# Token places written by indirect transfers into a DRAM table, a bias added by VectorE, and down products split for paired tiles only, in a Fourier-layer and mixture-of-experts kernel

## The chip, the cores and the metric

The kernel runs on one core of a Trainium2 chip. The metric is the time of one execution on the device in microseconds (us). The engines are named as in the profile: PE is TensorE with its matmuls, PEld its weight loads, DVE is VectorE, ACT is ScalarE, POOL is GpSimd, SP is SyncE, which here only issues transfers.

## The reference, cut to what matters

Eight sequences of 2496 rows and 256 columns go through a spectral layer: a real Fourier transform along the rows, a complex linear map with a bias, a soft threshold, and the transform back. The 19968 rows that come out then go, each for itself, through one of eight experts, chosen by the largest of eight logits.

```python
X = np.fft.rfft(x, axis=1)
Yr = Xr @ w_r - Xi @ w_i + b_r
Yi = Xr @ w_i + Xi @ w_r + b_i
Yr = np.sign(Yr) * np.maximum(np.abs(Yr) - lam, 0.0)   # Yi likewise, lam = 0.01
y = np.fft.irfft(Y, n=x.shape[1], axis=1)

logits = x @ w_gate                                    # x is y as (19968, 256)
e_idx = np.argmax(logits, axis=1)
gate_w = probs[np.arange(N), e_idx]                    # softmax of the logits
eom = 1.0 / (1.0 + np.exp(-(x @ w_output_gate)))
for e in range(E):
    mask = e_idx == e
    h = np.maximum(x[mask] @ w1[e], 0.0)               # 256 to 1024
    out[mask] = gate_w[mask, None] * eom[mask, e, None] * (h @ w2[e])
```

## The kernel before, in words

**Numbers.** Values are kept in float32 and split before a product into two float16 parts, high and low. A product of two such values is three float16 products (high-high, high-low, low-high), which is why so many steps come as a copy on ACT (the high part) and a subtraction on DVE or POOL (the low part).

**The Fourier part, batch by batch.** 2496 = 39 x 64. For each of 8 batches: `stage1` (L618) multiplies by the 39-point transform and L627/L628 split the result into `at`; `load_a` turns it round, by DMA transposes or by PE (`turn_a`, L661); `stage2` (L696) is the 64-point transform, split by L707/L708 into `xt` with a negated copy (L710 or L711). `mix` is the complex linear map: 24 matmuls (L726) into one bank of 512 columns, preceded by one matmul that puts the bias into that bank (L720: constant selector times the bias in two float16 parts, `b16`, made on POOL by L564 to L567, with the threshold already added). Two instructions make the soft threshold: ACT takes relu(y - 2 lam) from the bank (L741), DVE takes min(y, that) (L742), in the shifted form that the added threshold allows. The result `z` is split (copy L744 on ACT or L745 on POOL, subtraction L746 on POOL or DVE) and goes through the first step back (L756). There are 10 such `mix` blocks a batch, 80 in all. `inverse` transposes by DMA, `stage4` (L822) does the last step, and the rows go to a DRAM table `yd` together with a factor for each row (L834). `logits`, `gate` and `rank` (L867 to L960) pick each row's expert and its rank among that expert's rows.

**Expert weights.** While the batches run, `weights` reads the experts' matrices, splits them (L1017 to L1022) and stores them as float16 pairs in DRAM (`wd`).

**Routing, in two phases.** The tokens are laid out in tiles of 128 rows of one expert. Phase 0 makes the first 64 tiles out of the first four batches, as 32 pairs; phase 1 makes the other 99 single tiles once all batches are ranked. Each batch has 22 columns of 117 tokens. For a column, DVE writes two one-hot tables, `ol` (L1217: place within the tile, 117 x 128) and `ob` (L1221: which tile, times the token's number, 117 x 64 or 117 x 99), and one matmul (L1248) adds their product to a map of 128 places by 64 or 99 tiles in PSUM. `indices` (L1152 to L1180, DVE) turns the maps into `gidx`, the rows to fetch, and `sidx`, the rows to write. Phase 0 has 88 columns, phase 1 has 176.

**The experts.** For each tile POOL gathers 128 rows of `yd` by `gidx` (L1321, an indirect transfer), the rows are scaled and split (L382 to L393, L1335, L1340, L1341), turned by a DMA transpose, multiplied by the first matrix ("up", L1448: 48 matmuls a block, in four steps for a pair and two for a single tile), relu and split (L1458 on ACT, L1459 on DVE), multiplied by the second ("down", L1413: 24 matmuls a tile, in two halves, each as soon as its half of `hh` is there), scaled (L1430) and scattered to the output by `sidx` (L1433). `fetch` loads a block's 2 MB of weights into one of three buffers (L1307), in two parts, up and down, and each part only when the expert changes; a part is issued when the block three places earlier has done with it.

**What sets the order.** The kernel is recorded by a planner (`Issue`): each step is a generator that yields an engine, a rank, a duration and the instructions; whenever an engine is free in the plan, the waiting step of lowest rank is taken. Ranks and durations are written-out constants (`P`, `Z1`, `QV` and so on). The chip then executes each engine's instructions in just that order, each waiting by semaphores for what it needs. A list in a `yield` offers a step to two engines, and the first that is free in the plan takes it.

## Time and profile before

| | |
|---|---|
| three timed runs | median 1487.54 us (1483.97 to 1492.78) |
| the profiled execution | 1490.97 us, with a span of 1489.1 us from its first to its last instruction and a mean granted PE clock of 0.986 |
| PE busy | 1425.2 us, 96% of the span |
| DVE, ACT, POOL busy | 1023.4, 738.7 and 582.0 us |
| first expert product (L1448) | starts at 571.61 us |
| first single tile | up starts at 925.5 us |

A row of the profile's page names line, engine, operation, what is written and read, and a count; after the bar stand the busy time of the group, the mean duration of one in ns, and the time that the engine sat idle just before them, with what ended it. In a timeline a row is a start in us, a length, the instruction and how many follow each other; in brackets is the idle time before it. Matmuls overlap: one lasts about 0.27 us from its start to its end, but the next starts after about 0.11 us, so the pitch from one row's start to the next row's is what PE pays.

### The profile page before, as it was taken

What the parts mean: (1) busy time and instruction counts of PE and PEld (TensorE: products, weight loads), DVE (VectorE), ACT (ScalarE), POOL (GpSimd) and SP (SyncE); (2) the same over time, 40 slices, a digit from 0 to 9 for tenths busy, and PEclk for the clock granted to TensorE, in tenths of its full rate; (3) what the DMA queues carried; (4) which work ended last, traced back from release to release, by engine and by line L of the source; (5) the groups of instructions that cost most, each with busy time, mean ns of one, the idle gap of its engine ahead of it and who ended that gap; (6) DMA issues with size and microseconds to landing.
All of it is one profiled execution on the core that took longest, in us unless ns stands there. A gap on an engine that the chain in (4) does not pass through costs nothing. (4 is left out here: it accounts for less than half of the span.)

```text
span 1489.1 us, 42875 instructions
## 1 busy us (share of the span) xinstructions
PE 1425.2 (96%) x16464; PEld 1288.6 (87%) x16464; DVE 1023.4 (69%) x3167; ACT 738.7 (50%) x1415; POOL 582.0 (39%) x659
## 2 busy tenths in 40 slices
PE   5999999999989999999999999999999999999998
PEld 5998888898878777789998889889898988989898
DVE  4888778789999988789888865445454544545432
ACT  4777777777666655343333343333343333333332
POOL 2264645536354445333333343334333333333311
PEclk8999999999999999999999999999999999999999
DMA  7778989898777678978775778583847568386420
GB/s 191 175 166 222 219 224 220 216 210 209 188 193 187 157 207 198 260 194 234 220 235 158 205 228 273 133 237 80 235 115 194 152 158 225 86 238 196 110 51 23
DMA packets 294136, 276.39 MB, mean 186 GB/s; under 512 B 241859, under 2 KB 250426, under 8 KB 282155
## 3 DMA queue, kind: packets, MB, share of 16 engines
q1 hardware_dynamic: 277369, 229.59, 59.3%
q0 software_dynamic: 15872, 42.83, 10.2%
q8 instruction: 129, 2.11, 0.6%
q10 hardware_dynamic: 690, 1.24, 0.3%
q14 instruction: 76, 0.62, 0.1%
HBM read 337.35 MB, written 58.91 MB: 266 GB/s over the span
## 5 line engine op out<-in xcount | busy, mean ns | idle before, releaser
L1448 PE MATMUL ps<-eT,wbuf 128*128 128x128 f16 (+1 forms) x6288 | 485.0, 233 | 18.3 <-DMA wbuf<-wd 18.1
L1413 PE MATMUL ps<-wbuf,hh 128*128 128x256 f16 x3912 | 482.1, 275 | 1.9 <-issue 1.9
L1448 PEld LDWEIGHTS <-wbuf 128*128 128x128 f16 x6288 | 432.2, 98 | 44.3 <-DMA wbuf<-wd 20.9
L1413 PEld LDWEIGHTS <-hh 128*128 128x128 f16 x3912 | 376.1, 99 | 44.9 <-issue 2.2
L1459 DVE SCALAR_TENSOR_TENSOR hh<-ps,hh 128x512 f16<-128x512 f32 x326 | 224.8, 690 | 250.3 <-ACT hh L1458 201.8
L1458 ACT ACTIVATE hh<-ps 128x512 f16<-128x512 f32 x326 | 193.5, 594 | 296.3 <-PE ps L1448 277.2
L1433 POOL DMA_INDIRECT out<-o,sidx x163 | 164.2, 1007 | 304.8 <-ACT o L1430 111.4
L1321 POOL DMA_INDIRECT yg<-yd,gidx x163 | 160.4, 984 | 292.7 <-DVE yhl L1341 223.7
L726 PE MATMUL ps<-whl,xt 128*128 128x256 f16 x1920 | 227.2, 276 | 0.0
L726 PEld LDWEIGHTS <-xt 128*128 128x128 f16 x1920 | 190.1, 99 | 33.8 <-issue 1.3
L1340 ACT ACTIVATE yhl<-yg,ys 128x256 f16<-128x256 f32 x163 | 82.2, 505 | 183.2 <-DMA eT<-yhl 90.8
L1341 DVE SCALAR_TENSOR_TENSOR yhl<-yg,ys,yhl 128x256 f16<-128x256 f32 x163 | 78.5, 482 | 89.2 <-ACT yhl L1340 89.2
L1430 ACT ACTIVATE o<-ps,fac 128x256 f32<-128x256 f32 x163 | 77.0, 472 | 82.4 <-PE ps L1413 72.9
L746 POOL TENSOR_TENSOR zhl<-z,zhl 128x512 f16<-128x512 f32 x62 | 73.0, 1179 | 56.5 <-ACT zhl L744 52.4
L618 PE MATMUL ps<-f1t,x 117*128 117x120 f32 (+1 forms) x704 | 90.9, 287 | 0.0
L618 PEld LDWEIGHTS ps<-f1t,x 117*128 117x128 f32 (+1 forms) x704 | 87.8, 203 | 2.0 <-ACT at L627 0.6
L745 POOL CAST zhl<-z 128x512 f16<-128x512 f32 x47 | 29.7, 631 | 137.8 <-DVE z L742 83.5
L756 PE MATMUL ps<-gt,zhl 128*128 128x128 f16 x960 | 66.5, 219 | 10.2 <-POOL zhl L746 4.1
L756 PEld LDWEIGHTS <-zhl 128*128 128x128 f16 x960 | 58.5, 98 | 18.8 <-POOL zhl L746 4.9
L1221 DVE TENSOR_SCALAR ob<-t,blk,va 117x99 f16<-117x99 f16 (+1 forms) x264 | 71.7, 337 | 0.0
L741 ACT ACTIVATE zhl<-ps,sc 128x512 f32<-128x512 f32 x80 | 54.7, 684 | 30.3 <-PE ps L726 23.9
L822 PE MATMUL ps<-bdt,f4t 120*117 120x512 f16 x264 | 69.1, 379 | 0.4 <-ACT ste L773 0.3
(193 smaller groups left out, 1684.6 us busy)
## 6 DMA issues: line engine op xcount, KB each, us to landing
wbuf<-wd SPq DMA_DIRECT2D x262, 1024.0 KB
yd<-yt SPq DMA_DIRECT2D x120, 158.4 KB
x<-in_x SPq DMA_DIRECT2D x114, 156.0 KB
wr<-in_moe_w SPq DMA_DIRECT2D x32, 512.0 KB
wd<-wsp SPq DMA_DIRECT2D x64, 256.0 KB
yg<-yd,gidx POOLq DMA_INDIRECT x163
eT<-yhl SPq DMA_TRANSPOSE x163
out<-o,sidx POOLq DMA_INDIRECT x163
```

The lines of the kernel that those rows point to most:

```text
L618: T.matmul(pv[:, dh, :, m * j:m * j + m], xs[:k, j0 + j, 128 * dh:128 * dh + 128], fw, start=True, stop=True)
L726: T.matmul(yp[:, 256 * j:256 * j + 256], xt_[:, v, 2 * dh + j, 64 - 64 * u:192 - 64 * u], whl[:, dh, vw, 256 * u:256 * u + 256], start=Fal ...
L756: T.matmul(bv[:, j], zhl[:, vz, c:c + 128], gt[:, 2 * p + j, v], start=(n == 0), stop=(n == 2))
L1321: yield "G", r + 5.6 * t - 30, 1.0, lambda: G.indirect_dma_start(out=yg, out_offset=None, in_=src, in_offset=bass.IndirectOffsetOnAxis(ap= ...
L1340: yield "A", r - 10, 0.5, lambda: A.activation(yhl[:, 0], yg[:, :256], AF.Copy, scale=s)
L1341: yield "D", r - 10, 0.48, lambda: V.scalar_tensor_tensor(yhl[:, 1], yg[:, :256], s, yhl[:, 0], ALU.mult, ALU.subtract)
L1413: T.matmul(st["pt", t][1][:, :256], hh[:, v, fc, 128 * n:128 * n + 128], w[:, fc // 2, vw, fc % 2], start=(half == k == 0), stop=(half == ...
L1430: yield "A", r - DN, 0.47, lambda: A.activation(o, pt[:, :256], AF.Copy, scale=fac)
L1433: yield "G", r - DN, 1.0, lambda: G.indirect_dma_start(out=out, out_offset=bass.IndirectOffsetOnAxis(ap=sidx[:, t:t + 1], axis=0), in_=o, ...
L1448: T.matmul(pt[:, 128 * m * j:128 * m * (j + 1)], w[:, dh, g // 4, vw, 128 * (g % 4):128 * (g % 4) + 128], eT[:, :m, v, dh], start=(n == 0) ...
L1458: yield "A", r, 0.6, lambda: A.activation(hv[:, 0], pt, AF.Relu)
L1459: yield "D", r, 0.69, lambda: V.scalar_tensor_tensor(hv[:, 1], pt, 0.0, hv[:, 0], ALU.max, ALU.subtract)
```

## The change

1. **Bias.** The matmul L720 and its selector are gone, and so are POOL's two-part bias. DVE adds the bias, as float32, while it empties the bank (`z` = bank x 2^-7 + bias). As there is no shift any more, the soft threshold takes one more instruction: ACT makes relu(z - lam) into `c`, and then either DVE takes min(z + lam, `c`), or ACT makes relu(-z - lam) and POOL subtracts it from `c`.
2. **Phase 0 of the routing** (`SCAT`). DVE computes for each token the address of its place (`addr` = place x 64 + tile, or a number out of bounds for a token that phase 0 leaves out), and POOL issues 88 indirect transfers, one for each column, that write the tokens' numbers, 4 bytes each, into a table of 8192 numbers in DRAM, which was filled with "none" before. SP reads the table back into `sidx` when all have landed, and one DVE instruction makes `gidx`. For phase 0 there are no one-hot tables, no matmuls L1248 and no `indices`.
3. **Phase 1** still uses one-hot tables, but four columns are written by one DVE instruction each for `ol` and `ob`, and the token's number is multiplied in by a third, on DVE or POOL.
4. **Single tiles.** The halves of a tile's down product are issued as one step of 24 matmuls that waits for both halves of `hh`; a pair still has two halves. The ranks of single tiles' up and down steps move with that.
5. The tables of constants change (ranks and planned durations), the values table comes as float16 within another constant, and `z` and `zhl` are given out by free place rather than in turn.

```diff
-P = 68.49
+P = 68.76
-Z3 = 40.87
+Z3 = 32.19
...
+SCAT = (0,)
+SG = 1.0
...
-            G.tensor_scalar(bs, bias, sc[:, 0:1], sc[:, 1:2], ALU.mult, ALU.add)
-            G.tensor_copy(b16, bs)
-            for p in (32, 96):
-                G.tensor_tensor(b16[p:p + 32], bs[p:p + 32], b16[p:p + 32], ALU.subtract)
...
+        yield "G", r + 5, 0.5, lambda: G.tensor_scalar(bs, bias, sc[:, 0:1], 1.0, ALU.mult, ALU.mult)
...
-            T.matmul(yp.rearrange("p (a d) -> p a d", a=2), sel, st[b, "bs"].rearrange("p (o d) -> p o d", o=1).broadcast_to([128, 2, D]), start=True, stop=False)
...
-        i, yp = yield "P", r, 2.85, f, True
+        i, yp = yield "P", r, 2.64, f, True
...
-        yield "A", r - Z1, 0.69, lambda: A.activation(c, yp, AF.Relu, bias=sc[:, 2:3], scale=2.0 ** -7)
-        yield "D", r - Z1, 0.68, lambda: V.scalar_tensor_tensor(z, yp, 2.0 ** -7, c, ALU.mult, ALU.min)
+        yield "D", r - Z1, 0.68, lambda: V.scalar_tensor_tensor(two(z), two(yp), 2.0 ** -7, bs, ALU.mult, ALU.add)
         io.free(i)
+        yield "A", r - Z1, 0.68, lambda: A.activation(c, z, AF.Relu, bias=sc[:, 1:2])
...
+            A.activation(z, z, AF.Relu, bias=sc[:, 1:2], scale=-1.0)
+
+        yield [("D", r - Z1 + QD, 0.85, lambda: V.scalar_tensor_tensor(z, z, sc[:, 1:2], c, ALU.subtract, ALU.min)), ("A", r - Z1 + QA, 0.68, f)]
+        if way:
+            yield "G", r - Z1, 1.25, lambda: G.tensor_tensor(z, c, z, ALU.subtract)
...
+        V.tensor_scalar(t2[:, 1], t2[:, 1], -none, none - 1, ALU.mult, ALU.add)
+        yield
+        V.scalar_tensor_tensor(t2[:, 0], rlo[:, cs], float((T_A, T_B)[ph]), t2[:, 0], ALU.mult, ALU.add)
+        V.tensor_tensor(addr[:, cs], t2[:, 0], t2[:, 1], ALU.add)
...
+    def scatters(ph, r):
...
+        def f(c):
+            i = G.indirect_dma_start(out=tab[ph], out_offset=bass.IndirectOffsetOnAxis(ap=addr[:, c:c + 1], axis=0), in_=tok[:, c:c + 1], in_offset=None, bounds_check=128 * n - 1, oob_is_err=False).ins
+            tc.declare_no_dep(i, group=key, reason="places of different tokens differ")
...
+        for c in range((NA, B)[ph] * NQ):
+            yield "G", r, 1.0, lambda: f(c)
+            r += SG
+        yield 3.0
+
+        def g():
+            d = nc.sync.dma_start(sidx[:, t0:t0 + n], tab[ph].rearrange("(p t) o -> p (t o)", p=128)).ins
+            for i in all_:
+                tc.add_manual_dep(d, i.name, mybir.DependencyInfo(mybir.DependencyClass.Sync, mybir.DependencyReason.DATA), reason="the table is whole")
+
+        yield "S", r, 0.5, g
+        yield 2.0
+        yield "D", r, 0.4, lambda: V.scalar_tensor_tensor(gidx[:, t0:t0 + n], sidx[:, t0:t0 + n], none, sidx[:, t0:t0 + n], ALU.is_lt, ALU.mult)
...
-                    for j in range(m):
-                        V.tensor_scalar(ol[:, j], iota[:P3], rlo[:, c0 + j:c0 + j + 1], None, ALU.is_equal)
...
+                yield "D", r, 0.147 * m, lambda: V.tensor_tensor(ol[:, :, :m], iota[:P3, :, :m], bc(rlo, 128), ALU.is_equal)
+                yield "D", r, 0.115 * m, lambda: V.tensor_tensor(ob[:, :, :m], iota[:P3, :n, :m], bc(blk, n), ALU.is_equal)
...
+        yield either("D", r, 0.11 * m, "G", r + QO, 0.7, lambda e: e.tensor_tensor(ob[:, :, :m], ob[:, :, :m], vb, ALU.mult))
...
-            io.go(up(t, m, half, w, eT, ie, hh, r + UP * half))
+            io.go(up(t, m, half, w, eT, ie, hh, r + UP * half * (m - 1)))
...
-            io.go(down(t + i, m, i, w, hh, ih, r + (5.6 + UP * i) * m + DN))
+            io.go(down(t + i, m, i, w, hh, ih, r + (11.2 + 2 * UP * i + DN if m > 1 else 4)))
...
-        for half in range(2):
-            for i in range(m * half, m * half + m):
+        for half in range(m):
+            for i in range(2 * half, 2 * half + 2):
                 yield "hh", t0, i
```

The order of the built programs shows the two places that matter most. First, POOL's order around batch 6's bias, at the beginning of phase 0's tables; `zhl` and `z` belong to the mix, `wr` and `wsp` to the experts' weights, `yt` to the rows that go to `yd`. Before:

```order
L1020 TENSOR_SCALAR wr_5345<-wr_5345,swe_6362 128x512
L1021 TENSOR_TENSOR wsp_6372<-wr_5345,wsp_6372 128x512
L564 TENSOR_SCALAR bs_6293<-bias,sc_6292 128x256
L565 CAST b_6294<-bs_6293 128x256
L567 TENSOR_TENSOR b_6294<-bs_6293,b_6294 32x256 x2
L746 TENSOR_TENSOR zhl_6409<-z_6408,zhl_6409 128x512
L1020 TENSOR_SCALAR wr_5942<-wr_5942,swe_6362 128x512
L1021 TENSOR_TENSOR wsp_6472<-wr_5942,wsp_6472 128x512
L745 CAST zhl_6453<-z_6452 128x512
```

And of the changed program (L561 is the bias, L1181 a scatter into the table, L743 the new subtraction, L745 and L746 as before, L1022 and L1023 the weights, L834 as before):

```order
L1181 DMA tab_78<-tok,addr 8192x1
L561 TENSOR_SCALAR bs_6435<-bias,sc_6434 128x256
L1022 TENSOR_SCALAR wr_5515<-wr_5515,swe_6466 128x512
L1023 TENSOR_TENSOR wsp_6557<-wr_5515,wsp_6557 128x512
L1181 DMA tab_78<-tok,addr 8192x1 x2
L743 TENSOR_TENSOR z_6426<-zhl_6427,z_6426 128x512
L1181 DMA tab_78<-tok,addr 8192x1
L746 TENSOR_TENSOR zhl_6427<-z_6426,zhl_6427 128x512
L1181 DMA tab_78<-tok,addr 8192x1 x11
L743 TENSOR_TENSOR z_6824<-zhl_6825,z_6824 128x512
L834 COPY yt_135<-gf_6593 117x4
L745 CAST zhl_6825<-z_6824 128x512
```

The 88 scatters stand between POOL's other instructions, one to eleven at a time, in 44 runs, from here to the last batch's mix; behind the last of them SP's read of the table stands in SP's queue ahead of one store of weights, the first loads of expert weights and the last batch's rows. Second, ACT's order among the single tiles, which follows PE's (`hh` empties a bank of an up step, `o` one of a down product, `yhl` prepares a later tile). Before:

```order
L1458 ACTIVATE hh_9932<-ps_20505 128x512
L1340 ACTIVATE yhl_20571<-yg_19893,ys_20603 128x256
L1458 ACTIVATE hh_9932<-ps_20574 128x512
L1430 ACTIVATE o_20652<-ps_20555,fac_19228 128x256
L1458 ACTIVATE hh_9932<-ps_20627 128x512
L1340 ACTIVATE yhl_20693<-yg_20015,ys_20725 128x256
L1458 ACTIVATE hh_9932<-ps_20696 128x512
L1430 ACTIVATE o_20774<-ps_20677,fac_19350 128x256
```

And now:

```order
L1514 ACTIVATE hh_9860<-ps_20201 128x512
L1514 ACTIVATE hh_9860<-ps_20234 128x512
L1514 ACTIVATE hh_9914<-ps_20263 128x512
L1514 ACTIVATE hh_9914<-ps_20309 128x512
L1486 ACTIVATE o_20403<-ps_20337,fac_18963 128x256
L1398 ACTIVATE yhl_20367<-yg_19711,ys_20373 128x256
L1398 ACTIVATE yhl_20428<-yg_19771,ys_20438 128x256
L1486 ACTIVATE o_20471<-ps_20378,fac_19146 128x256
```

Before, the two up steps of a tile alternated with the two halves of the tile before it; now the four up steps of two tiles follow each other, and then the two tiles' down products.

More of the change, by code (lines that the diff above doesn't have):

```diff
@@ L294, in tile_fft_moe @@
     pools = {}
+    tab = [pd.tile([128 * n, 1], I32, name=f"tab{ph}") for ph, n in enumerate((T_A, T_B))]
     turn = {}
@@ L442, in tile_fft_moe @@
     G.memset(oh16, 0.0)
[L443 removed]
+    rlo = pc.tile([P3, NCOL], F16, name="rlo")
     rhi = pc.tile([P3, NCOL], F16, name="rhi")
     io = Issue(list(range(8)))
[L447 removed]
+    slots = {k: Slots(n) for k, n in dict(x=XR - 6, s1=S1, A=AN, xt=3, bt=1, bd=1, yt=YR, ol0=OL[0], wr=WR - 1, wsp=SR, ol1=OL[1], fac=12, dg=1, gL=1).items()}
     slots.update({k: Places(range(EARLY[k])) for k in EARLY})
[L449 removed]
+    slots.update(eT1=Places([]), hh1=Places([]), z=Places(range(2)), zhl=Places(range(ZR)))
     give = lambda k: io.give(slots[k])
@@ L1031, in tile_fft_moe @@
     eb = pc.tile([128, T_ALL], F32, name="eb")
-    blk = pc.tile([P3, NCOL], F32, name="blk")
+    blk = pc.tile([P3, NCOL], F16, name="blk")
     def prefix(src, name):
@@ L1205, in routing @@
         io.set("blocks", ph)
+        if ph in SCAT:
+            yield from scatters(ph, r)
         pool = (psm, pools.get("h"))[ph]
-        for b in range(nb):
+        for b in range(0 if ph in SCAT else nb):
             for q in range(0, NQ, CB):
@@ L1227, in routing @@
                 yield max(gap * m - 1.2, 0.0)
-        while st.get(("cols", ph), 0) < nb * NQ:
-            yield 1.0
-        yield from parts(indices(ph), "D", r, 0.6)
+        if ph not in SCAT:
+            while st.get(("cols", ph), 0) < nb * NQ:
+                yield 1.0
+            yield slots["gL"]
+            yield from parts(indices(ph), "D", r, 0.6)
+            give("gL")
+            for i in range(-(-nb // (512 // n))):
+                io.free(route["map", ph, i][0])
         io.set("ix", ph)
-        for i in range(-(-nb // (512 // n))):
-            io.free(route["map", ph, i][0])
         if ph == 0:
```

190 lines of the change are left out of this document (104 added, 86 removed).

## The prediction

> **What bounds the kernel now.** I read first the page's busy times, then the busy time of each engine in five stretches, then the waits of PE over the last stretch. The page:
>
> ```profile
> span 1489.1 us, 42875 instructions
> PE 1425.2 (96%) x16464; PEld 1288.6 (87%) x16464; DVE 1023.4 (69%) x3167; ACT 738.7 (50%) x1415; POOL 582.0 (39%) x659
> ```
>
> PE is busy 96% of the span, so the end moves only by PE work that goes and by PE's idle time, 63.9 us in all. The stretches show where that lies: batches before any routing table, batches with phase 0's tables, the last batch's end, pairs, single tiles. After the bounds and the length come busy times, the granted PE clock, the DMA share and GB/s.
>
> ```profile
> 40.00:383.40 343.40, 339.11 (x3929) 302.45 (x3928) 282.66 (x697) 256.50 (x485) 171.87 (x212) 1.00 0.86 206
> 383.40:541.30 157.90, 146.54 (x1613) 124.48 (x1611) 149.90 (x439) 100.24 (x191) 68.34 (x87) 0.97 0.74 184
> 541.30:571.40 30.10, 26.56 (x281) 21.78 (x279) 25.90 (x73) 20.87 (x45) 15.90 (x19) 1.00 0.70 217
> 571.40:917.00 345.60, 343.30 (x3268) 304.71 (x3267) 275.75 (x1072) 137.43 (x269) 129.18 (x135) 1.00 0.77 218
> 917.00:1489.10 572.10, 547.53 (x7244) 513.42 (x7241) 271.80 (x840) 205.70 (x397) 188.91 (x190) 0.98 0.56 152
> ```
>
> The first stretch loses 4.3 us, the pairs 2.3. Phase 0's tables lose 11.4 while DVE is busy 95% of the stretch; the single tiles lose 24.6 with every other engine under half busy. The waits of PE in the single tiles say for what:
>
> ```profile
> PE ps L1448 <- DMA wbuf<-wd: 18.1, 8, 3.2
> PE ps L1413 <- issue: 1.9, 2, 1.0
> ```
>
> So three quarters of that loss is eight waits for the next expert's weights.
>
> **The bias off PE.** PE's rows around one mix, each a start, a length and what follows:
>
> ```profile
> 41.73 0.38 PE L720 MATMUL ps<-b,t 128*128 128x512 f16 x1
> 41.95 2.78 PE L726 MATMUL ps<-whl,xt 128*128 128x256 f16 x24
> 44.57 0.61 PE L661 MATMUL ps<-t,at 128*128 128x128 f16 x8
> 45.01 0.83 PE L696 MATMUL ps<-ct,A 128*128 128x128 f16 x12
> 45.68 0.38 PE L720 MATMUL ps<-b,t 128*128 128x512 f16 x1
> ```
>
> Matmuls overlap, so the price is the step to the next start: 0.22 us for L720, not its 0.38. Eighty of them go: **-17.6**. The same rows give 2.62 us for a mix of 24 (0.109 each), 0.055 for a turning matmul and 0.056 for stage 2. The order has eight more turning matmuls, 280 for 272: **+0.4**.
>
> **Phase 0's tables off PE and DVE.** Groups of the second stretch; after the bar stand busy time, mean ns, and the idle time before them:
>
> ```profile
> L1248 PE MATMUL ps<-ob,ol 117*128 117x64 f16 x88 | 10.5, 191 | 7.5 <-DVE ob L1221 7.1
> L1221 DVE TENSOR_SCALAR ob<-t,blk,va 117x64 f16<-117x64 f16 x88 | 28.7, 388 | 0.0
> L1217 DVE TENSOR_SCALAR ol<-t,rlo 117x128 f16<-117x128 f16 x88 | 23.4, 326 | 0.0
> ```
>
> With the 88 matmuls go 7.5 us of waiting for DVE and whatever they occupied, at most their busy 10.5: between 7.5 and 18.0. By the step of 0.055 for 128 columns above, 88 of them occupied some 4.5 of the 10.5; **-12**. DVE gets back 52.1 us there.
>
> **A dearer threshold.** The nearest rows to the new instructions (counts, then ns min/median/max; L742 from 40 to 383 us, the others over the whole run):
>
> ```profile
> L742 DVE SCALAR_TENSOR_TENSOR z<-ps,zhl x53: 669/690/693, 45.6 to 378.2; 128x512 f32<-128x512 f32 x53
> L1022 DVE SCALAR_TENSOR_TENSOR wsp<-wr,swe,wsp x14: 736/904/1540, 106.7 to 523.9; 128x512 f16<-128x512 f32 x14
> L744 ACT ACTIVATE zhl<-z x33: 613/629/667, 46.9 to 563.7; 128x512 f16<-128x512 f32 x33
> L746 POOL TENSOR_TENSOR zhl<-z,zhl x62: 1148/1158/1522, 47.6 to 569.1; 128x512 f16<-128x512 f32 x62
> L746 DVE TENSOR_TENSOR zhl<-z,zhl x18: 678/693/1660, 80.8 to 564.9; 128x512 f16<-128x512 f32 x18
> ```
>
> The bias addition takes L742's place at its 0.68. The second half of the threshold is new: in the order 41 of the 80 go to DVE and 39 to ACT with a subtraction on POOL. DVE's min reads two SBUF operands as L1022 does; I take 0.95, a little over its median. Of the 80 mixes 53, two thirds, have L742 in the first stretch: 27 x 0.95 = 26 us more on DVE; and of the low-part subtractions 33 are DVE's in the new order, not 18, ten of the fifteen there, at 0.69 to 1.0: 9 more. DVE goes from 282.7 to 317 us of a stretch that shrinks by 53 x 0.22 = 11.7 to 332: 95%, as full as it was in the second stretch. There PE's idle time beside that before L1248 was 11.4 - 7.5 = 3.9 us. ACT's 39 further instructions (0.63 each, 24.5) lie in its idle 87 us there. A mix's chain also grows by one instruction, which the waiting banks must cover. The cost lies between 0, if PE always has another batch's work to take, and 16, if it waits 0.3 us, about half of an L742, at each of the 53; **+7**, from the 4 us in 158 that the second stretch shows at the same filling (8.5 in 343, 4 more than now) and 3 for the longer chain. In the second stretch DVE loses 52 and gains some 13: 111 of about 141, so it is no longer the one that is late. What is late next is POOL.
>
> **The scatters on POOL.** The nearest rows are the gathers, also 128 rows by index; the first four rows give start, length, and in brackets the idle time before them, the fifth all gathers from 650 to 850 us, and the sixth the busy times there.
>
> ```profile
> 558.26 1.17 POOL L746 TENSOR_TENSOR zhl<-z,zhl 128x512 f16<-128x512 f32 x1
> 559.58 0.97 POOL L1321 DMA_INDIRECT yg<-yd,gidx  x1 [0.16 <-DMA wbuf<-wd]
> 560.86 0.95 POOL L1321 DMA_INDIRECT yg<-yd,gidx  x1 [0.30 <-issue]
> 562.12 1.21 POOL L1321 DMA_INDIRECT yg<-yd,gidx  x1 [0.30 <-issue]
> L1321 POOL DMA_INDIRECT yg<-yd,gidx x36: 967/981/1034, 653.5 to 846.6; - x36
> 650.00:850.00 200.00, 199.71 (x1926) 179.15 (x1924) 176.83 (x710) 75.79 (x146) 72.45 (x73) 1.00 0.69 205
> ```
>
> One indirect transfer holds POOL for 0.98 us whatever is written, with 0.15 ahead of a first and 0.30 between two in a row. The order puts the 88 scatters in 44 runs: 88 x 0.98 + 44 x 0.15 + 44 x 0.30 = 106 us. Between the first and the last of them stand POOL's other instructions, priced by these groups of the second stretch:
>
> ```profile
> L1021 POOL TENSOR_TENSOR wsp<-wr,wsp 128x512 f16<-128x512 f32 x17 | 20.3, 1195 | 1.4
> L746 POOL TENSOR_TENSOR zhl<-z,zhl 128x512 f16<-128x512 f32 x15 | 17.4, 1157 | 8.1 <-ACT zhl L744 7.3
> L1020 POOL TENSOR_SCALAR wr<-wr,swe 128x512 f32<-128x512 f32 x17 | 12.7, 746 | 14.5 <-ACT wsp L1017 14.0
> L745 POOL CAST zhl<-z 128x512 f16<-128x512 f32 x11 | 6.9, 629 | 39.6 <-DVE z L742 32.7 <-PE ps L822 6.0 <-PE ps L756 0.7
> ```
>
> Fifteen subtractions of the mix (17.4), five casts (3.1), nine pairs for the weights (17.5), two more weight parts (2.4) and fifteen small ones (4.5): 45 us. With 5 for the last landing, the table's reading and `gidx`, the chain lasts 156. PE's work between the same places: 157.9 less 12 and less 20 biases (4.4) is 141.5, and by the order more matmuls stand between them now, 51 of the mix (5.6), 30 of stage 2 (1.7) and others (1.6): about 150. So POOL is 6 us late on this estimate: **+6**, between 0 and 20 (a pitch of 0.16 more, one launch's idle time, for each scatter). Who waits for a late POOL: each mix's step back L756, through the low part, and at the end the pairs' first gathers. Behind SP's read of the table wait a store of weights, the first expert weights and the last batch's rows; behind `gidx` on DVE, the last batch's emptying of banks. A scatter also waits, by the order's semaphores, for the eighth before it; at 1.2 us each that leaves it 9.6 us. The nearest transfers, the last two scatters of the output, land much sooner (start, length):
>
> ```profile
> 1477.46 2.60 DMA out<-o,sidx
> 1482.76 2.13 DMA out<-o,sidx
> ```
>
> The Trainium skill, page "SBUF — State Buffer", section "SBUF: two separate sides", has VectorE and GpSimd share a port that one holds for a whole instruction, and has transfers issued by GpSimd take some 3.1 us rather than 0.62 beside a VectorE copy. The trace disagrees: 967 to 1034 ns for 36 gathers with DVE busy 88% of the time. By the page's figure the scatters' chain would be an estimated 88 x 3.1 + 50 = 323 us, 173 late. As a mechanism priced from rows it stands in the third rival below.
>
> **Phase 1.** Its edits fall into 571 to 917, where PE is busy 343.3 of 345.6, and its maps are needed only when the singles begin. DVE has 70 us free there to cover them: nothing. If a table came late, the pitch of a single tile, some 5.8 us (572 / 99), would be the price.
>
> **Single tiles.** A change of expert, as SP, PE and the clock show it:
>
> ```profile
> 975.42 0.36 SPq L1307 DMA_DIRECT2D wbuf<-wd  x1
> 983.66 1.50 PE L1448 MATMUL ps<-eT,wbuf 128*128 128x128 f16 x24
> 997.14 1.07 PE L1448 MATMUL ps<-eT,wbuf 128*128 128x128 f16 x16 [2.71 <-DMA wbuf<-wd]
> 1064.00:1066.00 2.00, 2.00 (x21) 1.69 (x19) 1.16 (x3) 1.70 (x4) 1.01 (x1) 0.63 0.98 396
> 1066.00:1068.00 2.00, 2.00 (x15) 1.57 (x13) 1.59 (x8) 0.56 (x2) 0.98 (x1) 0.52 0.64 165
> ```
>
> The load issued at 975.42 serves the wait that ends at 997.14: 21.7 us for three blocks' parts. After a wait the clock falls to 0.52 to 0.63, which costs 4 x 0.425 = 1.7 us, seen after five of the eight: 18.1 + 8.5 = 26 in all. The buffers come free by PE's order. Before, up and down halves alternate, and the lead of the first load is 8.2 us. In the new order four ups and then two downs follow each other, so that the up part comes free two halves earlier: by 24 or 32 matmuls of 0.09 to 0.11, a lead of 10.4 to 11.3, against stalls of 2.3 in the mean (18.1 / 8). So they shrink to nothing or to 2 us each, as the down parts come later in turn. Between 0 and 26 off; **-8**, a third. The relu of two tiles in a row has ACT's free 64% to hide in. At the very end two tiles now finish 2.6 us apart (24 matmuls), and each one's scatter takes an issue of 1.0 and 2.1 to 2.6 to land: **+1**.
>
> **The sum.** -17.6 + 0.4 - 12 + 7 + 6 - 8 + 1 = -23.2. The profiled execution took 1490.97, 3.4 above the median of the runs: 1467.8, or **1464** against 1487.5.
>
> **Rivals.** *Nothing in the way*: POOL keeps pace, DVE's filling costs 2, and more than half of the weight waits goes (-15): -17.6 + 0.4 - 15 + 2 - 15 + 1 = -44, **1443**. For it: POOL's lateness is 4% of its chain, and the lead grows by more than the mean wait. Against: the down parts come later by what the up parts gain. *Handed back*: DVE at 95% and POOL in series hold each mix. With the scatters' pitch at 1.45, their chain is 22 us longer, which takes back nearly all: **1486**. For it: both engines stand in one chain with every mix, and L746 has maxima of 1.5 on POOL and 1.7 on DVE. *Slower, by the scatters*: POOL is held at each scatter by DVE, or by the eighth before it, whose 117 writes of 4 bytes are slow to land. The trace has no write of 4 bytes. It decides from a pitch of 1.56: 106 / 88 = 1.20, and 31 us more (the 23 gained and the 7.4 of the bound below) over 88. If each scatter waits out one DVE instruction of 0.68, the pitch is 1.88, 60 us more than at 1.20; PE has other batches' work for some 9 of it: 1464 + 51 = **1515**. For it: nothing in 650 to 850. Against: those gathers beside a DVE that is 88% busy. *No effect*: the order shows that L720 and phase 0's L1248 are gone, so hardly.
>
> **How the numbers follow.** What a measurement of this kernel can tell from no change is about 0.5%, 7.4 us: faster is under 1480, slower over 1495. Chances: the forecast (1452 to 1478) 0.47, nothing in the way 0.18, handed back 0.19, slower by the scatters 0.14, no effect 0.02. Faster is the first two and 0.01 of handed back, 0.66; the same is 0.16 of handed back and no effect, 0.18; slower is 0.14 and the last 0.02 of handed back, 0.16. The range goes from the first rival, 1443, to 1492, above handed back; the slower case is left out, and what lies below 1443.
>
> **What would show it.** Right: no idle time of PE over 8 us before 383; scatters at about 1.2 us pitch, with POOL some 90 to 95% busy between the first and the last; PE's idle time around the first gathers under 10; weight waits of 8 to 12 us in sum; the singles' stretch shorter by 5 to 10. Wrong: PE waiting for `zhl` low parts or for DVE's `z` by tens of us; scatters above 1.5 us; the first pair later than 560 us; weight waits as before.

## The result, and the profile after

| | before | after |
|---|---|---|
| four timed runs each, median | 1489.14 us | 1550.98 us (1546.42 to 1554.95) |
| ratio | | 1.0419, 95% interval 1.0389 to 1.0449 |
| span of the profiled execution | 1489.1 us | 1553.2 us |

The change made the kernel slower by 62 us. The page of the changed kernel, as of before:

```profile
span 1553.2 us, 42607 instructions
PE 1436.4 (92%) x16304; PEld 1294.5 (83%) x16304; DVE 1011.6 (65%) x2790; ACT 763.5 (49%) x1471; POOL 722.1 (46%) x774
```

PE has less to do, yet is busy 11 us longer, at a granted clock of 0.965 for 0.986, and its idle time went from 63.9 to 116.8 us. To see where, the span is cut at the first pair's first matmul and at the first single tile: batches from 350 us, pairs with what is left of the batches, single tiles. Busy times of PE, PEld, DVE, ACT and POOL follow the length; then come PE's clock, the DMA share and GB/s. Before:

```profile
350.00:571.60 221.60, 204.89 (x2288) 173.74 (x2286) 207.31 (x594) 144.21 (x279) 104.50 (x132) 0.98 0.76 190
571.60:925.50 353.90, 351.60 (x3345) 312.24 (x3344) 281.02 (x1088) 140.95 (x276) 132.28 (x139) 1.00 0.77 220
925.50:1489.10 563.60, 539.03 (x7166) 505.79 (x7163) 266.33 (x823) 201.99 (x389) 185.61 (x187) 0.98 0.55 150
```

After:

```profile
350.00:598.00 248.00, 204.31 (x2079) 170.50 (x2077) 191.24 (x442) 159.73 (x309) 184.00 (x193) 0.88 0.70 168
598.00:987.40 389.40, 371.04 (x3372) 326.15 (x3369) 261.24 (x849) 143.74 (x282) 168.70 (x177) 0.96 0.71 203
987.40:1553.20 565.80, 536.88 (x7166) 502.88 (x7163) 266.19 (x823) 199.58 (x389) 183.56 (x186) 0.99 0.55 149
```

The first pair comes 26 us later, the pairs take 36 us more, the single tiles 2. In the first stretch DVE is no longer full (77% for 94%), and POOL has taken its place. From the first scatter to the last it is busy 140.5 of 178.4 us, and another 21.6 are the 0.15 to 0.3 us ahead of each scatter, 91% in sum:

```profile
382.00:560.40 178.40, 151.15 (x1545) 127.69 (x1543) 130.08 (x279) 115.27 (x221) 140.45 (x143) 0.89 0.69 156
```

```profile
L1181 POOL DMA_INDIRECT tab<-tok,addr x88 | 93.6, 1063 | 21.6 <-issue 20.2
```

What PE waits for from 350 to 598 us, with the sum, the count and the longest in us:

```profile
PE ps L756 <- ACT z L739: 6.3, 1, 6.3
PE ps L756 <- issue: 6.1, 9, 1.5
PE ps L715 <- issue: 5.8, 8, 1.0
PE ps L822 <- issue: 4.6, 3, 2.8
```

"Issue" is idle time for which the trace shows no reason. In pieces of over 0.25 us it sums to 27 us over the span; before it was 3.

### The profile page after: what moved, and what is told of

It is laid out like the page before. It is cut to its first block, busy times and chain, and to the rows that moved or that the text cites. A ratio compares the mean times of both kernels' runs of the same rounds, so it can differ in the third digit from the quotient of the medians.

```text
span 1553.2 us, 42607 instructions
## 1 busy us (share of the span) xinstructions
PE 1436.4 (92%) x16304; PEld 1294.5 (83%) x16304; DVE 1011.6 (65%) x2790; ACT 763.5 (49%) x1471; POOL 722.1 (46%) x774
## 5 line engine op out<-in xcount | busy, mean ns | idle before, releaser
L1504 PE MATMUL ps<-eT,wbuf 128*128 128x128 f16 (+1 forms) x6288 | 469.1, 233 | 11.9 <-DMA wbuf<-wd 7.6
L1470 PE MATMUL ps<-wbuf,hh 128*128 128x256 f16 x3912 | 461.6, 274 | 12.0 <-issue 5.9
L1504 PEld LDWEIGHTS <-wbuf 128*128 128x128 f16 x6288 | 423.6, 98 | 37.8 <-DMA wbuf<-wd 8.9
L1470 PEld LDWEIGHTS <-hh 128*128 128x128 f16 x3912 | 381.7, 99 | 60.8 <-issue 10.3
L715 PE MATMUL ps<-whl,xt 128*128 128x256 f16 x1920 | 233.8, 280 | 8.3 <-issue 5.8
L1181 POOL DMA_INDIRECT tab<-tok,addr x88 | 93.6, 1063 | 21.6 <-issue 20.2
L756 PE MATMUL ps<-gt,zhl 128*128 128x128 f16 x960 | 71.6, 226 | 20.9 <-ACT z L739 6.3
L743 POOL TENSOR_TENSOR z<-zhl,z 128x512 f32<-128x512 f32 x39 | 50.6, 1299 | 80.4 <-ACT z L739 54.7
L822 PE MATMUL ps<-bdt,f4t 120*117 120x512 f16 x264 | 71.8, 396 | 5.1 <-issue 4.6
L687 PE MATMUL ps<-ct,A 128*128 128x128 f16 x960 | 69.9, 225 | 3.0 <-issue 2.0
L382 DVE TENSOR_REDUCE ym<-yg 128x1 f32<-128x256 f32 x163 | 66.5, 410 | 6.1 <-DMA yg<-yd,gidx 6.1
```

The source lines that it names most:

```text
L715: T.matmul(yp[:, 256 * j:256 * j + 256], xt_[:, v, 2 * dh + j, 64 - 64 * u:192 - 64 * u], whl[:, dh, vw, 256 * u:256 * u + 256], start=(n ...
L756: T.matmul(bv[:, j], zhl[:, vz, c:c + 128], gt[:, 2 * p + j, v], start=(n == 0), stop=(n == 2))
L1181: i = G.indirect_dma_start(out=tab[ph], out_offset=bass.IndirectOffsetOnAxis(ap=addr[:, c:c + 1], axis=0), in_=tok[:, c:c + 1], in_offset= ...
L1470: T.matmul(st["pt", t][1][:, :256], hh[:, v, fc, 128 * n:128 * n + 128], w[:, fc // 2, vw, fc % 2], start=(fc == k == 0), stop=(fc == 7 an ...
L1504: T.matmul(pt[:, 128 * m * j:128 * m * (j + 1)], w[:, dh, g // 4, vw, 128 * (g % 4):128 * (g % 4) + 128], eT[:, :m, v, dh], start=(n == 0) ...
```

## The experiments

The theories, as the expectations number them: **1**, the scatters are the loss, either (1a) because PE's instructions come late while POOL issues a long run of indirect transfers, or (1b) because POOL is late with its other work; **2**, the dearer threshold on ACT, DVE and POOL; **3**, the order that the new constants give.

Times are medians; the kernel before took 1486 to 1490 us beside every set. The sets ran on different chips, which turned out to matter: the first result and two sets (E1 to E4, E13 to E16) came from chips on which PE has such unexplained idle time, three sets (E5 to E8, E9 to E12, E17 and E18) from chips on which no run shows more than the 1.4 us of E8. The changed kernel itself ran on one of these three, in E12, and shows none. Below they are called chips with and without **slow stretches**.

**E1, E14, E18: phase 0's tables by one-hot products again.** The scatters are gone, all else is as changed.

```
-SCAT = (0,)
+SCAT = ()
```

> The changed kernel with phase 0's tables made by one-hot products again; everything else as changed. Theory 1 (the scatters are the loss, by whatever way): of the 62 us lost between the two kernels, 50 to 60 come back, some 1490 to 1500 us. Theory 2 (the dearer threshold on ACT, DVE and POOL is the loss): DVE gets its 52 us of one-hot tables on top of the dearer threshold, so no better than now, 1545 to 1575. Theory 3 (the new order by the tables of constants): within 15 us of now, 1536 to 1551.

> The changed kernel with phase 0's tables by one-hot products, as run before, beside it on the same chip. If POOL's pace is a cost of its own, 10 to 20 us less than the changed kernel where PE has no slow stretches (first pair at 567 for 583), and 30 to 35 less where it has. If the slow stretches are all that the scatters cost, within 6 us of the changed kernel where there are none.

> The changed kernel with phase 0's tables by one-hot products, once more, as the witness of the kind of chip. With slow stretches 1513 to 1528 as before. Without them, its 7 us of such idle time and the lowered clock go: 1500 to 1512, against the 1516 of the changed kernel without them, which leaves the scatters' own cost at 4 to 16.

Measured: 1515.9 and 1523.8 us on the chips with slow stretches (with the scatters 1551.0 in the first result and 1551.8 beside the second), 1502.4 on a chip without. So neither "all from the scatters" nor "none": 28 to 35 us go with them where there are slow stretches, and with 15 us over the kernel before the rest of the change is no gain even where there are none.

**E2, E16: the runs of scatters broken up.** Same order; POOL does four small instructions after every fourth scatter of a run.

```
+            if io.grun % 4 == 0:      # scatters in a row so far
+                for _ in range(4):
+                    G.tensor_scalar(sp, f1t, 1.0, 0.0, ALU.mult, ALU.add)
```

> The changed kernel in the same order, with four small POOL instructions (about 1.2 us) after every fourth scatter of a run, nine times. Theory 1a (PE's instructions come late while POOL issues five or more indirect transfers in a row): of the 27 us in which PE waits for nothing that the trace shows, those beside the scatters (about 17) go, and the lowered clock after them; 1525 to 1538 us, and no such idle time before 560 us but one or two us. Theory 1b (POOL is simply late with 88 scatters): POOL is 11 us later, so 1551 to 1562.

> The changed kernel with 1.2 us of small POOL work after every fourth scatter of a run, as run before, beside it on the same chip. Where PE has no slow stretches the spacing has nothing to mend and makes POOL 11 us later: 3 to 14 us more than the changed kernel, if POOL sets the pace, and no more than 3 if it does not. Where it has them, 3 to 10 less, as before.

Measured: 1546.4 (5 less than the changed kernel) and 1551.6 (the same, where 3 to 10 less was expected). In E2 the idle time called "issue" fell from 27 to 19 us in all, and 9.6 of the 19 are one piece near 440 us that is no slow stretch: ACT waits 10.5 us there for POOL's subtraction (L747 in E2, L743 in the changed kernel), which stands behind scatters and small instructions, and PE goes on just after ACT. So the label covers such waits too. The time did not follow the rest: the time that theory 1a gave was missed; what the spacing saved, POOL's lateness took.

**E3, E15: the old bias and threshold, with the scatters.** L720 and the two-step threshold are as in the kernel before.

```
+            T.matmul(yp.rearrange("p (a d) -> p a d", a=2), sel, ..., start=True, stop=False)
...
+        yield "A", r - Z1, 0.69, lambda: A.activation(c, yp, AF.Relu, bias=sc[:, 2:3], scale=2.0 ** -7)
+        yield "D", r - Z1, 0.68, lambda: V.scalar_tensor_tensor(z, yp, 2.0 ** -7, c, ALU.mult, ALU.min)
+        io.free(i)
```

> The changed kernel with the bias by the matmul and the threshold in two instructions as before, the scatters kept. Theory 1 (scatters): the bias costs PE its 17.6 us again, less what a lighter DVE, ACT and POOL give back; 1545 to 1570. Theory 2 (threshold): 30 us or more come back, 1520 or less.

> The changed kernel with the bias by the matmul and the two-step threshold, scatters kept, as run before, beside it on the same chip. If the dearer threshold eats what the bias matmuls gave (17.6 us), within 6 us of the changed kernel; if the bias is a net gain, 10 to 18 us more; if a net loss, 8 or more less.

Measured: 1561.8 and 1566.7, 11 and 15 us more than the changed kernel. With the scatters in place, going back gains nothing: it costs most of the 17.6 us. The ranks and planned durations stay those of the changed kernel here, which were set for the new threshold.

**E4: the old starting rank of the pairs.**

```
-RT = -22.4
+RT = 0.74
```

> The changed kernel with one constant as before: the rank at which the pairs' steps start, 0.74 for -22.4, so that the last batch's steps come ahead of the first pairs' as they did. Theory 3 (order): the waits from 585 to 670 us (some 17 us) go, 1530 to 1540. Theories 1 and 2: within 6 us of 1551.

Measured: 1533.1, 18 us less than the first result. The matmuls of the last batch's ranking end at 639 us for 670, and the wait of 6.3 us for L739 shown above and one of 5.7 at the ranking are gone, with one of 6.0 for a copy on POOL in their place. The time is that of theory 3. But E4's unexplained idle time is also smaller, 18 us for 27, so not all of the 18 us need be the constant's, and no run changes it alone on a chip without slow stretches.

**E5, E6, E7, E17: further scatters in the kernel before.** In E5 and E17 eight at a time, in E6 two, in E7 plain POOL work of the same length instead.

```
             yield "G", r + 5.6 * t - 30, 1.0, ...   # the tile's gather
+            if 12 <= t < 56 and t % 4 == 0:
+                yield "G", r + 5.6 * t - 29, 1.28 * 8, extra
```

> The kernel before, with 88 further scatters of 4 bytes that nobody reads, among the pairs (where PE waits for nothing), in eleven groups of eight. Theory 1a (PE's instructions come late in a long run): idle time of PE for which the trace shows no reason appears at each group, 2 to 5 us of it and a lowered clock behind, 30 to 70 us in sum: 1520 to 1560. Theory 1b (only what waits for POOL is late): the gathers run several tiles ahead, so at most 1 us a group, 1487 to 1498.

> The same 88 further scatters in 44 groups of two. Theory 1a: no group is long enough, within 8 us of the kernel before, 1482 to 1497. If it is the number of scatters and not the length of a run that costs, as much as with groups of eight.

> The kernel before, with eleven stretches of about 10 us of plain POOL work (32 small instructions each) in place of the groups of eight. Theory 1a: POOL computes but issues no transfer, so PE loses nothing, 1482 to 1497. Theory 1b: as with the groups of eight.

> The kernel before with eleven groups of eight further scatters among the pairs, as run before on a chip where PE showed no slow stretches. The one-hot variant beside it tells which kind of chip this is, by its run of seven indirect transfers near 905 us (3.7 us of idle PE time for which the trace shows no reason, twice, on chips with slow stretches). On such a chip: if long runs of indirect transfers make the stretches, several of the groups show 3 us or more, 25 us or more in sum, and 1565 to 1610 us; if they need something else that only the changed kernel has, none, and 1545 to 1560. On a chip without: 1545 to 1560 again.

Measured: 1549.7, 1509.3, 1558.9 and 1545.7. E5 lies in the range of theory 1a, but for another reason: on neither chip is there one piece of unexplained idle time, in runs of up to 15 indirect transfers. Plain POOL work costs as much. PE waits for DVE's one-hot tables, E5 first, E7 second:

```profile
PE ps L1249 <- DVE ob L1222: 20.5, 13, 3.9
```

```profile
PE ps L1248 <- DVE ob L1221: 34.5, 15, 5.4
```

and DVE waits in its own order for rows that POOL fetched late, again E5 and E7:

```profile
DVE ym L383 <- DMA yg<-yd,gidx: 38.4, 12, 5.8
```

```profile
DVE ym L382 <- DMA yg<-yd,gidx: 43.2, 10, 8.0
```

So theory 1b is right in kind, and its estimate of 1 us a group was wrong: an engine that is 10 us late in one piece stops those that have a step behind it in their order. E6 spreads the same scatters and loses 23 us, 7 of them at the very end (last section). Together with the gathers its groups of two still stand in runs of up to 17 in a row, so E6 is no test of short runs.

**E8: what is left of the change without scatters, phase 1's tables and the starting rank.** One-hot tables a column at a time in both phases; the bias by VectorE, the single tiles' order and the other constants stay.

```
+RT = 0.74
+CB = 3
+SCAT = ()
...
+                    for j in range(m):
+                        V.tensor_scalar(ol[:, j], iota[:P3], rlo[:, c0 + j:c0 + j + 1], None, ALU.is_equal)
...
+                        V.tensor_scalar(ob[:, j], iota[:P3, :n], blk[:, c0 + j:c0 + j + 1], va32[:, c0 + j:c0 + j + 1], ALU.is_equal, ALU.mult)
```

> The changed kernel with one-hot products one column at a time in both phases (three columns prepared at a time for room) and the pairs' starting rank 0.74 as before; so the bias by VectorE, the single tiles' order and the other constants remain of the change. Theory 1 with 3 (scatters, phase 1's tables and the starting rank are the loss): the 17.6 us of bias matmuls come through less what DVE's tables meet on a dearer threshold, 1470 to 1495. Theory 2 (the threshold): 1505 or more.

Measured: 1511.7, in the range of theory 2. DVE is 94% busy in the first stretch, which lasts until 601 us, and PE waits for the tables as before, and longer:

```profile
350.00:601.40 251.40, 207.72 (x2187) 176.26 (x2185) 237.19 (x615) 158.14 (x297) 140.63 (x162) 0.90 0.69 169
```

```profile
PE ps L1315 <- DVE ob L1285: 12.3, 15, 2.2
```

**E9: half of the scatters.**

```
         for c in range((NA, B)[ph] * NQ):
-            yield "G", r, 1.0, lambda: f(c)
+            if c % 2 == 0:
+                yield "G", r, 1.0, lambda: f(c)
```

> The changed kernel with every second scatter left out, so that half of phase 0's tokens are not placed (their places stay empty). Theory 1b (POOL sets the pace while it issues the scatters: 177 us from the first to the last, where PE's own work is about 150): 44 times 1.28 = 56 us less for POOL, and the first pair 25 to 35 us earlier, at 563 to 573 for 598; 1515 to 1528. If PE's slow stretches for which the trace shows no reason were the cost, they go with the long runs and the gain is about the same; the place tells: 1b has PE's waits go all over 382 to 560. Theory 2 (threshold): the same time, 1545 to 1555.

Measured: 1498.3, against 1516.0 of the changed kernel on the same chip (E12). The first pair starts at 571.2 for 582.8: the 44 scatters are worth 12 us there, half of what theory 1b gave. Another 4 lie at the very end.

**E10: the order of the single tiles alone, in the kernel before.** The down steps' rank is 4.8 where the change has 4; four ups and two downs alternate as in the change.

```
-            io.go(up(t, m, half, w, eT, ie, hh, r + UP * half))
+            io.go(up(t, m, half, w, eT, ie, hh, r + UP * half * (m - 1)))
...
-            io.go(down(t + i, m, i, w, hh, ih, r + (5.6 + UP * i) * m + DN))
+            io.go(down(t + i, m, i, w, hh, ih, r + (11.2 + 2 * UP * i + DN if m > 1 else 4.8)))
...
-        for half in range(2):
-            for i in range(m * half, m * half + m):
+        for half in range(m):
+            for i in range(2 * half, 2 * half + 2):
```

> The kernel before with the change's order of the single tiles alone (four up steps of two tiles, then two whole down products). Prediction's term: the weight waits fall by a third, 8 us less, 1476 to 1483; if the order gains nothing, 1484 to 1491. The stretch of the single tiles tells: 559 us before.

Measured: 1465.9 us, ratio 0.987 (0.984 to 0.990) to the kernel before: the one version that beats both. Its single tiles, and their wait for weights:

```profile
921.80:1460.90 539.10, 531.08 (x7166) 500.38 (x7164) 268.39 (x823) 201.54 (x389) 184.53 (x186) 1.00 0.57 157
```

```profile
PE ps L1448 <- DMA wbuf<-wd: 0.3, 1, 0.3
```

563.6 us became 539.1, the eight waits of 18.1 us became one of 0.3, and the clock is 1.00 throughout.

**E11: phase 1's tables a column at a time, with the scatters and the old starting rank.** The edit of E8 with `SCAT = (0,)`.

> The changed kernel with the starting rank 0.74, and phase 1's tables one column at a time, three columns prepared together, multiplied and compared by one DVE instruction as before. Against 1533 with the starting rank alone: if the change of phase 1's tables costs PE (its matmuls there read columns four apart, 91 ns a step for 47, and wait for POOL's multiplication), 8 to 20 us less, 1513 to 1525, and the second phase's indices are ready before 870 us; if it costs nothing, 1528 to 1538.

Measured: 1509.8 for 1533.1 with the starting rank alone, but E4 ran on a chip with slow stretches. On E11's own chip the changed kernel took 1516.0 (E12), so that the tables and the starting rank, taken back together, give 6 us there. In the pairs' stretch E4 had only 2 us of unexplained idle time: E4, then E11.

```profile
594.80:971.90 377.10, 366.70 (x3369) 324.88 (x3368) 259.32 (x848) 142.90 (x280) 165.36 (x172) 0.98 0.74 208
```

```profile
592.00:947.10 355.10, 352.43 (x3344) 312.73 (x3345) 280.10 (x1082) 141.54 (x274) 130.65 (x136) 1.00 0.76 220
```

22 us less, and the length of before (353.9). E12 has 374.2 there, but its first pair starts at 582.8 for E11's 592.0, so that half of what the stretch gains is lost ahead of it. The columns four apart cost PE itself: four one-hot matmuls and the start of the next row, before and in the changed kernel (E12):

```profile
703.29 0.35 PE L1248 MATMUL ps<-ob,ol 117*128 117x99 f16 x4
703.48 1.47 PE L1448 MATMUL ps<-eT,wbuf 128*128 128x256 f16 x12
```

```profile
780.95 0.54 PE L1306 MATMUL ps<-ob,ol 117*128 117x99 f16 x4
781.31 1.49 PE L1504 MATMUL ps<-eT,wbuf 128*128 128x256 f16 x12
```

0.36 us for 0.19, 44 times: 7.5 us; in E11 the step from one to the next is that of before. Of E4's other 14 us some 7 are PE's busy time at a clock of 0.98 for 1.00, and 8 are idle time: 3.8 for POOL's multiplication, and 4.1 for expert weights, which the tables do not touch.

**E12, E13: the changed kernel again.**

> The changed kernel once more, to see whether the 27 us of idle PE time for which the trace shows no reason belong to the kernel: if so, 20 us or more again at the same places and 1546 to 1555; if they come and go, fewer, at about the same time if they lie beside waits for POOL anyway, or some 25 us less if they are the cost.

> The changed kernel again, timed beside the next three on one chip. Where PE's slow stretches (idle time for which the trace shows no reason, beside five or more indirect transfers in a row) are absent, 1512 to 1520 as in the one look at it; where they are there, 1546 to 1555. Either way the trace shows which: none, or some 27 us.

Measured: 1516.0 in a single execution on a chip without slow stretches, 1551.8 on one with them. There the label "issue" sums to 37 us, but two pieces of it, 6.2 and 5.5, end just behind ACT's copy that follows L743 on POOL, like the one in E2. The same instructions in the same order differ at one place like this. The first profile, beside a run of eleven scatters on POOL; L822 stops after three matmuls:

```profile
397.42 0.84 PE L822 MATMUL ps<-bdt,f4t 120*117 120x512 f16 x3
401.00 0.81 PE L822 MATMUL ps<-bdt,f4t 120*117 120x512 f16 x3 [2.75 <-issue]
402.71 1.44 PE L756 MATMUL ps<-gt,zhl 128*128 128x128 f16 x12 [0.90 <-issue]
405.61 1.44 PE L756 MATMUL ps<-gt,zhl 128*128 128x128 f16 x12 [1.46 <-issue]
```

E12, beside the same eleven scatters:

```profile
396.36 1.49 PE L822 MATMUL ps<-bdt,f4t 120*117 120x512 f16 x6
397.88 1.50 PE L756 MATMUL ps<-gt,zhl 128*128 128x128 f16 x24
399.22 0.81 PE L822 MATMUL ps<-bdt,f4t 120*117 120x512 f16 x3
399.87 0.83 PE L756 MATMUL ps<-gt,zhl 128*128 128x128 f16 x12
```

E12's stretches, to be held against the two tables at the top:

```profile
350.00:582.80 232.80, 196.66 (x2072) 166.28 (x2071) 192.00 (x443) 159.25 (x309) 185.46 (x192) 0.90 0.77 178
582.80:957.00 374.20, 364.02 (x3372) 323.96 (x3370) 259.67 (x848) 142.49 (x282) 165.50 (x172) 0.99 0.74 209
957.00:1514.20 557.20, 532.22 (x7166) 500.67 (x7163) 269.04 (x823) 202.05 (x389) 188.24 (x190) 0.99 0.57 152
```

Of the 64 us between the profiles, 39 are the difference between the two executions of the changed kernel (15 before the first pair, 15 in the pairs, 9 in the single tiles), and 25 are the change where there are no slow stretches: +11 before the first pair, +20 in the pairs, -6 in the single tiles.

## Why the prediction was wrong

It forecast 1464 and a range to 1492; 1551 lies outside, and the sign was wrong. Even without the slow stretches the kernel takes 1516.

By stretches, E12 against the kernel before, in us:

| | the forecast's terms | measured |
|---|---|---|
| up to the first pair | -17.6 + 0.4 - 12 + 7 + 6 = -16 | +11 |
| pairs | 0 | +20 |
| single tiles and end | -8 + 1 = -7 | -6 |

So two steps failed. The first is the overlap ahead of the first pair: PE was to have other batches' work while DVE and POOL were late, so that threshold and scatters cost 13 us together. With the other three terms as forecast they come to 40, whatever the new ranks add included. The 50th mix still starts its last matmul 9 us earlier than before (342 for 351 us); the time is lost behind it, and a first pair later than 560 us, which the prediction named as a sign of being wrong, is there (582.8). Some 12 of the missing 27 us go with the scatters: E18, without them, has its first pair at 570.3, and E9, with half, at 571.2. The second is phase 1 at nothing.

Step by step, by E12 where no other is named:

- **The bias off PE (-17.6): right.** L720 is gone, the 50th mix is 9 us early, and E3 and E15, where L720 returns, pay 11 and 15 us.
- **A dearer threshold (+7 before 383 us, 0 to 16): inside its range there, but not by DVE's filling.** PE's idle time from 40 to 383 us went from 4.3 to 16.4 in the first profile, +12 (15.5 in E12; the prediction's own limit was 8), with DVE at 89% where 95% was forecast:

```profile
40.00:383.40 343.40, 327.04 (x3790) 293.83 (x3788) 304.77 (x704) 258.89 (x494) 200.42 (x230) 0.98 0.88 200
```

  More than half of it lies in the last 33 us, mostly before the first scatter (381 us). E12, then E15, where the old threshold is back under the same ranks:

```profile
350.00:383.40 33.40, 24.77 (x285) 20.11 (x284) 31.94 (x81) 20.46 (x42) 20.15 (x23) 0.85 0.73 176
```

```profile
350.00:383.40 33.40, 33.25 (x420) 29.03 (x419) 32.58 (x85) 25.16 (x50) 21.36 (x27) 1.00 0.95 205
```

  PE idles 8.6 us in E12, as it does without scatters (8.4 in E18), and 0.2 in E15, with DVE as full in both; before it was 1.8. E12 waits there for DVE's L413 (4.5) and L746 (3.3). E15's batches run some 15 us later, so the two do not hold quite the same work. And that ACT's 39 further instructions "lie in its idle 87 us there" counted their time and not their place: in half of the mixes the chain now runs ACT, ACT, POOL and then often ACT again, for the copy (40 of the 80); that copy waits in ACT's order with everything behind it, banks to be emptied included.
- **The scatters on POOL (+6, 0 to 20): the mechanism right, the size too small, and only half of it seen.** The scatters' price was near: 94.4 us and 21.6 of idle time ahead of them, 116 for 106. Their chain, from the first scatter to `gidx`, took 172 us in E12 for the 156 of the forecast:

```profile
L1181 POOL DMA_INDIRECT tab<-tok,addr x88: 982/996/1520, 381.2 to 546.4; - x88
```

```profile
L1198 DVE SCALAR_TENSOR_TENSOR gidx<-sidx x1: 216/216/216, 553.7 to 553.7; 128x64 int32<-128x64 int32 x1
```

  That it ends late is one thing; the other is that mixes' subtractions stand behind runs of up to eleven scatters. E12's waits of ACT and of PE from 350 to 583 us:

```profile
ACT zhl L744 <- POOL z L743: 23.1, 10, 4.7
```

```profile
PE ps L756 <- ACT zhl L744: 12.5, 4, 6.0
PE ps L417 <- DVE dg L413: 7.6, 3, 4.2
```

  The rival "handed back" named this chain. It gave it 0.19 and 1486.
- **Phase 0's tables off PE and DVE (-12): not to be had apart from the scatters.** The matmuls and the tables are gone, but the scatters are about even with one-hot products a column at a time (E11 and E8 differ only in them and are 1510 and 1512) and 14 us dearer than those four columns at a time (E18, 1502; E12, 1516), between chips without slow stretches in both pairs.
- **Phase 1 ("nothing"): wrong, some 12 of the pairs' +20.** The argument was that its tables are not yet needed and that DVE has room for them. It did not price the matmuls on the new layout (7.5 us more) and did not ask what the new multiplication on POOL waits behind (4.0). The maps were done at 900 us for 849. Another 5.3 of the 20 are a wait at the last batch's ranking (L940), which E4, with the old starting rank, does not have; some 4 are a clock of 0.99, an estimate from 364 us of busy time.
- **Single tiles (-8): too small, by three times where they are alone.** The weight waits fell from 18.1 to 10.3 us in the first profile and 5.6 in E12, whose stretch is 6 shorter, or 14 without the longer end below; alone, in E10, to 0.3, which with the clock is 24 us. The forecast had the lead of the up parts right, and a loss by the down parts that E10 does not show.
- **The tail (+1): wrong, +7.4,** from a cause that no term had (last section).
- **The slow stretches: no term, 39 us between the two profiles.** The prediction quotes their sign, a wait for "issue" of 1.9 us, and passes over it.
- **The starting rank and the other constants: no term.** E4 gives the rank 18 us on a chip with slow stretches; on E12's chip rank and phase 1's tables give 6 together (E11), so the 18 and the 12 above do not add up. The prediction read the order at two places only.

The rival on the slower side was right in sign and wrong in mechanism: in runs the scatters kept the 1.28 us from one to the next and were not held by DVE, so that E12's 1516 beside its 1515 says nothing for it. The Trainium skill's 3.1 us for transfers that GpSimd issues beside a VectorE copy (page "SBUF — State Buffer", section "SBUF: two separate sides") is not seen here either: L1181 has a median of 996 ns and a maximum of 1520.

What stays open: how much of the 46 us between E8 and E10 (51 between the profiles, 32 of these ahead of the first pair) is the dearer threshold on a full DVE and how much the ranks and planned durations that were changed with it. E3 and E15 take back the threshold alone, but with the scatters and on chips with slow stretches, and gain nothing; no run has the new threshold under all the old ranks. Open is also what makes the slow stretches; E12, the one view of the changed kernel without them, is a single execution. On those chips they were seen beside long runs of indirect transfers in every set, but long runs in the kernel before were tried only on chips without them (E5, E6, E17).

## What to carry to other kernels

Ask of each instruction that moves to another engine not only whether that engine has time, but what stands ahead of it in that engine's order, and who stands behind the engine that waits for it: 10 us of POOL work in one piece, of whatever kind, cost the kernel before 5 to 7 us each time, where POOL was 37% busy. Take a bundle of edits apart: one of these five, alone, gains 21 us. And look at a second execution on another chip before explaining idle time for which the trace shows no reason.

## What the runs showed of the hardware

- **More indirect transfers make the end longer.** POOL's last drain (ns min/median/max of three) in the kernel before, the changed kernel, and E9 with half of the scatters:

```profile
L1512 POOLq DRAIN  x3: 51/103/2887, 1485.4 to 1488.9; - x3
```

```profile
L1569 POOLq DRAIN  x3: 51/103/10257, 1542.1 to 1552.9; - x3
```

```profile
L1570 POOLq DRAIN  x3: 51/103/6337, 1489.4 to 1496.3; - x3
```

  88 further transfers make it 7.4 us longer, 44 make it 3.5, 0.08 us each, some 900 us after the last of them. E5 and E6, with 88 in the kernel before, show 10.27 and 10.35; E7, with POOL work instead, 2.89.
- **Slow stretches of PE on some chips.** Its matmuls and weight loads then start one by one, about 0.7 us apart, while POOL, DVE and ACT run at their usual lengths. In the first profile most of the 27 us came beside runs of five to eleven indirect transfers, in E1 beside its longest run, of nine (3.7 of 7 us), and on other chips not at all. The kernel before, with one run of five, lost 1.9 us to it.
- **A matmul that reads columns eight bytes apart** took twice the step of one that reads them side by side (0.09 us for 0.047, 117x99 by 117x128): 0.09 in E12 and E18, 0.048 in E8 and E11, where the tables lie side by side again.
